# One decode step of attention and MLP: TensorE in a loop of four turns with one V buffer, and announced jumps at two engines' ends

## The chip, the cores and the metric

The kernel runs on one core of a Trainium2 chip. The metric is device microseconds (us) of one execution, median of several. A core has five engines with an instruction stream each: TensorE (PE; its weight loads are listed apart as PEld), VectorE (DVE), ScalarE (ACT), GpSimd (POOL) and SyncE (SP). Transfers between main memory (HBM) and the core's memory (SBUF, 128 partitions) are issued by SyncE or ScalarE and carried out by 16 DMA engines. TensorE writes into eight banks of PSUM. The engines are held together by semaphores alone.

## The reference

One token (Sq = 1) for a batch of 2, model width 448. Layer norm of x; q = xn wq for 16 heads of width 256; attention of two query heads per key/value head (8 of them) over the last 2048 positions of a cache of 8192; output projection wo (4096 to 448). Beside it an MLP on xn (448 to 1792, ReLU, back to 448) whose SiLU gates the attention's output:

```python
s = A(layernorm(x), k_cache, v_cache, wq, wo)     # softmax(q k^T / 16) v, then @ wo
g = silu(relu(layernorm(x) @ w1) @ w2)
return x + s * g
```

All inputs are bf16. K and V windows are 16.8 MB each, wq and wo 3.67 MB each, w1 and w2 1.61 MB each: 44.1 MB to read for little arithmetic.

## The kernel before

**Tiling.** The 16 pairs of batch and key/value head are worked on in four units u of four heads (one batch, half of the heads). A unit's K is one load of 4 MB into `ub[i]`, 128 partitions of 32 KB, a partition holding 64 neighbouring positions of one head; its V likewise. The three buffers `ub[0..2]` take K and V in rotation (`place`, L259).

**A unit's work.** `do_turn` (L268): VectorE transposes K in 32 x 32 blocks, four instructions from `ub` into `kt`. `do_S` (L301): four matmuls put a mask into the bank `sbk`, 32 more add the scores. `do_chain` (L318): VectorE's row maximum, a transpose on TensorE, maximum over groups, broadcast by another matmul, ScalarE's exponential, a transpose on VectorE, 16 small matmuls into `pbk`, and ScalarE's copy to `pt`. `do_sum` (L346): the sums. `do_PV` (L351): 32 matmuls of V by `pt` into `obk`. `do_o` (L361): division by the sum, four matmuls that bring o into columns, a copy into `at_exp`.

**Weights.** wq and w1 have 448 rows. `wq_src` and `w1_src` (L191, L192) cut every row into two halves and lay the 896 halves on all 128 partitions, seven (`SLOTS`) each; `xg`, `par8` and `xr` make the matching arrangement of xn, with zeros where a half doesn't belong. `do_q_mm` (L277) is 28 matmuls into `obk`, `do_q` (L287) brings q for all units into `qz`; `do_H` (L378) is 28 matmuls of w1, `do_F` (L394) 56 of w2 and the gate. wo goes into wq's place (`wqo`) when q is done, in four loads of 20, 8, 2 and 2 rows per partition (`WO_PARTS`), and 128 matmuls into `wbk` consume it in that order at the end.

**Order.** `_Prog` (L23) collects instructions in a list per engine, in the order of the calls in L409 to L483; `run` (L40) writes the lists out straight, with a wait where an instruction needs a later value of a semaphore than its engine has seen. SyncE issues all large loads in one order: wq's first seventh, k0, rest of wq, k1, v0, k2, v1, k3, v2, w1, v3, w2, wo, and then 15 tiny loads `d_probe` (L449), for which it waits at last (L451). A load waits for its buffer: k2 for turn 0, v1 for turn 1, k3 for PV(0), v2 for turn 2, v3 for PV(1). TensorE's order at the units is S(0), S(1), PV(0), S(2), PV(1), PV(2), S(3), H, PV(3), with the chains' small matmuls between; then the two last matmuls of o (L463), F and wo. ScalarE issues the output's transfer and waits for it.

Of the kernel before, what the change touches and what calls it, by code (L numbers as in the profile page):

```python
# [14 lines left out]
class _Op:  # L15
    __slots__ = ("eng", "fn", "deps", "dma", "needed", "value", "sem")

    def __init__(self, eng, fn, deps, dma):
        self.eng, self.fn, self.deps, self.dma = eng, fn, deps, dma
        self.needed, self.value, self.sem = dma, 0, None  # L20


class _Prog:  # L23


    def __init__(self, nc, es):
        self.nc, self.es = nc, es
        self.lists = {PE: [], DVE: [], ACTE: [], SP: [], POOL: []}

    def op(self, eng, fn, deps=()):  # L30
        o = _Op(eng, fn, [d for d in deps if d is not None], False)
        self.lists[eng].append(o)
        return o

    def dma(self, eng, dst, src, deps=()):
        o = _Op(eng, lambda e: e.dma_start(dst, src), [d for d in deps if d is not None], True)  # L36
        self.lists[eng].append(o)
        return o

    def run(self):  # L40
        n = 0
        for ops in self.lists.values():
            for o in ops:
                for d in o.deps:
                    d.needed = True
        for e, ops in self.lists.items():
            sem, count = self.es.enter_context(self.nc.semaphore(f"s_{e}")), 0
            for o in ops:
                if o.dma:
                    n += 1  # L50
                    o.sem, o.value = self.es.enter_context(self.nc.semaphore(f"d_{n}")), 16
                elif o.needed:
                    count += 1
                    o.sem, o.value = sem, count

        def emit(eng, ops):
            seen = {}
            for o in ops:
# [4 lines left out]
                for key, (sem, value) in want.items():  # L63
                    if value > seen.get(key, 0):
                        eng.wait_ge(sem, value)
                        seen[key] = value
                made = o.fn(eng) if o.fn else None
                if o.needed:
                    made.then_inc(o.sem, 16 if o.dma else 1)

        for name, e in (("sync", SP), ("scalar", ACTE), ("gpsimd", POOL), ("vector", DVE), ("tensor", PE)):
            emit(getattr(self.nc, name), self.lists[e])


def bass_recurrent_scan__sliding_block_cached__dense_activation_relu__decode_kernel(
# [22 lines left out]
    NU = 4  # L98
    NT = 64
    UW = NT * DH  # L100
    SLOTS = 7
    HC = HD // 2
    FC = DFF // 2
    WO_PARTS = [20, 8, 2, 2]
    NCOL = D // 4

    es = contextlib.ExitStack()
    with es:
# [5 lines left out]
        def psum(name, shape, dt):  # L114
            return es.enter_context(nc.psum_tensor(name, shape, dt))
# [7 lines left out]
        one_f = named("one_f", [128, 1], F32)  # L123
        par8 = named("par8", [128, 8], F32)
        par2 = named("par2", [128, 2], F32)
        qmask = named("qmask", [128, 4], F32)
        fold = named("fold", [128, 32], BF)
        gsum = named("gsum", [128, 128], F32)
        amask = named("amask", [128, 32], BF)
        x_sb = named("x_sb", [128, D], BF)  # L130
        xg = named("xg", [128, 9 * 128], BF)
# [4 lines left out]
        xr = named("xr", [128, SLOTS * 4], BF)  # L136
        q_n = named("q_n", [128, 512], BF)
        q_t = named("q_t", [128, 512], BF)
        rep4 = named("rep4", [128, 512], BF)
        m8 = named("m8", [1, 8], F32)  # L140
        qz = named("qz", [128, NU * 8 * 32], BF)
        fold8 = named("fold8", [128, 8], F32)
        xr2 = named("xr2", [128, SLOTS * 32], BF)
        h_n = named("h_n", [128, FC // 4], BF)
        h_t = named("h_t", [128, FC // 4], BF)
# [5 lines left out]
        probe = named("probe", [16, 16 * 15], BF)  # L151
        rm = named("rm", [128, 1], F32)
        mrow = named("mrow", [128, 128], F32)
# [5 lines left out]
        pt = [named(f"pt{i}", [128, 512], BF) for i in range(2)]  # L159
# [3 lines left out]
        wqo = named("wqo", [128, 32 * D], BF)  # L163
        assert SLOTS * HC <= 32 * D
        ub = [named(f"ub{i}", [128, UW], BF) for i in range(3)]
        kt = named("kt", [128, UW], BF)
        w1_sb = named("w1_sb", [128, SLOTS * FC], BF)
        w2_sb = named("w2_sb", [128, 14 * D], BF)

        sbk = psum("sbk", [128, 512], F32)  # L170
        pbk = psum("pbk", [128, 512], F32)
        obk = psum("obk", [128, 512], F32)
        fbk = psum("fbk", [128, 512], F32)
        wbk = psum("wbk", [128, 512], F32)
        mbk = psum("mbk", [128, 512], F32)
        hbk = psum("hbk", [128, 512], F32)

        def mbk_ap(lo, n, rows=128):
            return view(mbk, lo, [[1, n]], n=rows)

        def kv_src(u, cache):
            hg, b = divmod(u, 2)
            a = cache[b, 4 * hg:4 * hg + 4, SK - W:SK, :]
            return a.rearrange("h (p t) d -> p h (t d)", t=NT)
# [5 lines left out]

        wq_src = A_wq.rearrange("r (hf c) -> (r hf) c", hf=2).rearrange("(p s) c -> p (s c)", s=SLOTS)  # L191
        w1_src = B_w1.rearrange("r (hf c) -> (r hf) c", hf=2).rearrange("(p s) c -> p (s c)", s=SLOTS)  # L192
        w2_src = B_w2.rearrange("(hf p j) n -> p hf (j n)", hf=2, j=7)
# [5 lines left out]
            base=0, pattern=[[-1, 128]], channel_multiplier=1), [i0])  # L199
        i1 = pr.op(POOL, lambda e: e.memset(ident_f[:, :], 0.0), [p_id])  # L200
# [3 lines left out]
        p_one = pr.op(POOL, lambda e: e.memset(one_f[:, :], 1.0), [p_idf])  # L204
        p_at = pr.op(POOL, lambda e: e.memset(at2[:, :], 0.0))
        p_x2 = pr.op(POOL, lambda e: e.memset(xr2[:, :], 0.0))
# [7 lines left out]
        for e2 in range(2):  # L214
            v_xn = pr.op(DVE, lambda e, e2=e2: e.tensor_scalar(
                out=view(xg, 128 - 127 * e2, [[256, 4], [128, 2], [2, 64]], n=B),
                in0=view(x_sb, 3 * e2, [[1, 4], [0, 2], [SLOTS, 64]], n=B),
                scalar1=st2[0:B, 0:1], scalar2=rstd[0:B, 0:1],
                op0=ALU.subtract, op1=ALU.mult), [v_rs])
        v_par = pr.op(DVE, lambda e: e.tensor_reduce(  # L220
            out=par2[:, :], in_=view(ident, 0, [[1, 2], [2, 64]]), axis=AX.X, op=ALU.add), [p_id])
        v_par8 = pr.op(DVE, lambda e: e.tensor_copy(
            view(par8, 0, [[2, 4], [1, 2]]), view(par2, 0, [[0, 4], [1, 2]])), [v_par])
        v_qm = pr.op(DVE, lambda e: e.tensor_reduce(
            out=qmask[:, :], in_=view(ident, 0, [[32, 4], [1, 32]]), axis=AX.X, op=ALU.add))
# [5 lines left out]
        for i in range(4):  # L231
# [5 lines left out]
        v_gs = pr.op(DVE, lambda e: e.tensor_copy(  # L237
            view(gsum, 0, [[8, 16], [1, 8]]), view(fold8, 0, [[0, 16], [1, 8]])), [v_fold8])
        v_am = pr.op(DVE, lambda e: e.tensor_scalar(
            out=view(amask, 0, [[8, 4], [2, 4], [1, 2]]), in0=view(ident, 0, [[0, 4], [1, 4], [0, 2]]),  # L240
            scalar1=-1.0, scalar2=BIG, op0=ALU.add, op1=ALU.mult), [p_id])

# [4 lines left out]
        for s in range(SLOTS):  # L247
            m_xr = pr.op(PE, mm(mbk_ap(2 * s, 2), xg[0:B, 128 * s + 128:128 * s + 256], ident[0:B, 0:B], s == 0),
# [265 lines left out]
```

## Time and profile before

| what | value |
|---|---|
| median of three runs | 111.34 us (111.2 to 111.41) |
| the profiled execution | 111.39 us, span 109.9 us |
| data read from HBM | 44.11 MB, 401 GB/s over the span |
| mean granted clock of TensorE | 0.761 |
| K transposes on VectorE | 16, 35.6 us, 2279 ns each |
| K loads, V loads | 4 + 4, 4096 KB each |
| matmuls, weight loads | 625 and 625 |

The span runs from the first to the last instruction. A row of a group names line, engine, operation, output from input, count, busy us and mean ns of one, then the idle time before it and what ended it. Nearly all matmuls have L244, the helper's line, so they are told apart by their tiles: `sbk` scores, `obk` PV (and q), `pbk` probabilities, `hbk` and `fbk` MLP, `wbk` output projection, `mbk` small ones. In the slices every digit is the busy share of a fortieth of the span in tenths. The chain that ended last is followed backwards and is no sum of all work.

### The profile page before, as it was taken

To read this page: it belongs to the slowest core of one execution; us is meant where nothing else is said; L and a number is where in the kernel's file an instruction comes from. 1 tells how busy PE (TensorE), PEld (TensorE's weight loads), DVE (VectorE), ACT (ScalarE), POOL (GpSimd) and SP (SyncE) were. 2 spreads that over 40 slices of the span, in tenths; PEclk is the share of its full clock that TensorE was granted. 3 is DMA by queue.
4 is the path that set the end of the run, shared out by engine and by line. 5 is a ranking of instruction groups with operands and counts; after the bars stand their busy time and mean duration, and the time that the engine had idled before them with its cause. 6 is when DMAs were issued, how large, how long until landed. Compare 5 with 4: busy or idle time off the path is not lost.

```text
span 109.9 us, 1444 instructions
## 1 busy us (share of the span) xinstructions
PE 41.1 (37%) x625; PEld 19.2 (17%) x625; DVE 58.0 (53%) x85; ACT 11.0 (10%) x21; POOL 2.5 (2%) x12
## 2 busy tenths in 40 slices
PE   0120000275921302982310059620049913575281
PEld 0000000012211101321210024210013512213270
DVE  1870089937068697016389941348995245123401
ACT  2900000014011200000310000040000022000000
POOL 6200000000000000000000000000000000000000
PEclk9999999999995555599855556995555996569555
DMA  3989999998999899989999998999899988999930
GB/s 59 514 382 465 441 429 429 441 465 382 417 513 405 382 447 489 394 382 465 468 394 405 477 453 382 423 477 429 359 423 482 465 376 373 432 428 416 400 116 7
DMA packets 2706, 44.21 MB, mean 402 GB/s; under 512 B 522, under 2 KB 780, under 8 KB 1292
## 3 DMA queue, kind: packets, MB, share of 16 engines
q1 hardware_dynamic: 2672, 44.11, 94.4%
q8 instruction: 5, 0.08, 0.3%
q10 hardware_dynamic: 28, 0.01, 0.0%
q14 instruction: 1, 0.01, 0.0%
HBM read 44.11 MB, written 0.00 MB: 401 GB/s over the span
## 4 chain that ended last, share of the span: by engine, by line
DMA 49%; PE 22%; DVE 20%; issue 3%; SPq 2%; ACT 1%
DMA wqo<-in_A_wo_dram 31%; DMA wqo<-in_A_wq_dram 18%; DVE kt L273 14%; PE sbk L244 11%; PE obk L244 6%; PE mbk L244 2%; SPq L36 2%; PE wbk L244 1%; DVE ptd L334 1%; DVE rm L319 1%; PE pbk L244 1%; ACT e_sb L329 1%; PE mbk L321 1%; DVE o_sb L363 1%; ACT q_n L288 1%
## 5 line engine op out<-in xcount | busy, mean ns | idle before, releaser
L273 DVE STREAM_TRANSPOSE kt<-ub 128x2048 f32<-128x2048 f32 x16 | 35.6, 2279 | 6.4 <-DMA ub<-in_A_k_cache_dram 6.4
L244 PE MATMUL obk<-ub,pt 128*16 128x512 bf16 x128 | 11.0, 503 | 8.2 <-DMA ub<-in_A_v_cache_dram 8.2
L244 PE MATMUL sbk<-kt,qz 128*32 128x512 bf16 x128 | 12.6, 556 | 0.0
L244 PE MATMUL obk<-wqo,xr 128*4 128x512 bf16 x28 | 3.3, 619 | 15.4 <-DMA wqo<-in_A_wq_dram 13.4
L244 PE MATMUL sbk<-ident,amask 128*32 128x512 bf16 x16 | 2.4, 585 | 16.5 <-DVE kt L273 15.9
L363 DVE TENSOR_SCALAR o_sb<-obk,rs 128x512 bf16<-128x512 f32 x4 | 3.0, 742 | 10.3 <-PE obk L244 10.3
L329 ACT ACTIVATE e_sb<-sbk,bias 128x512 bf16<-128x512 f32 x4 | 2.7, 687 | 53.5 <-DVE bias L328 53.5
L319 DVE TENSOR_REDUCE rm<-sbk 128x1 f32<-128x512 f32 x4 | 2.8, 689 | 9.8 <-PE sbk L244 9.8
L244 PEld LDWEIGHTS obk<-ub,pt 128*16 128x16 bf16 x128 | 3.7, 108 | 14.0 <-DMA ub<-in_A_v_cache_dram 8.4
L244 PEld LDWEIGHTS sbk<-kt,qz 128*32 128x32 bf16 x128 | 4.6, 131 | 6.8 <-issue 6.1
L244 PE MATMUL pbk<-ptd,ident 128*32 128x128 bf16 x64 | 2.0, 264 | 8.5 <-DVE ptd L334 8.5
L244 PE MATMUL wbk<-wqo,at 128*17 128x112 bf16 x128 | 3.4, 296 | 3.0 <-DMA wqo<-in_A_wo_dram 3.0
L334 DVE STREAM_TRANSPOSE ptd<-e_sb 128x512 bf16<-128x512 bf16 x4 | 2.8, 702 | 2.5 <-ACT e_sb L329 2.5
L244 PEld LDWEIGHTS obk<-wqo,xr 128*4 128x4 bf16 x28 | 0.8, 108 | 17.2 <-DMA wqo<-in_A_wq_dram 13.9
L244 PEld LDWEIGHTS sbk<-ident,amask 128*32 128x32 bf16 x16 | 0.5, 113 | 17.1 <-DVE kt L273 16.4
L244 PEld LDWEIGHTS wbk<-wqo,at 128*17 128x17 bf16 x128 | 2.8, 131 | 3.5 <-DVE g_sb L406 2.8
L343 ACT ACTIVATE pt<-pbk 128x512 bf16<-128x512 f32 x4 | 2.4, 598 | 6.7 <-PE pbk L244 6.7
L349 DVE RECIPROCAL rs<-mbk 128x1 f32<-128x1 f32 x4 | 0.7, 169 | 4.1 <-PE mbk L244 4.1
L477 DVE TENSOR_TENSOR tmp<-wbk,g_sb 128x112 f32<-128x112 f32 x1 | 0.3, 274 | 4.7 <-PE wbk L244 4.7
L244 PEld LDWEIGHTS pbk<-ptd,ident 128*32 128x32 bf16 x64 | 1.2, 112 | 8.8 <-DVE ptd L334 8.8
L288 ACT ACTIVATE q_n<-obk 128x512 bf16<-128x512 f32 x1 | 0.6, 597 | 18.8 <-PE obk L244 18.8
L244 PE MATMUL mbk<-one_f,mrow 1*128 1x1 f32 x8 | 1.5, 256 | 2.5 <-DVE mrow L325 2.5
(66 smaller groups left out, 35.9 us busy)
## 6 DMA issues: line engine op xcount, KB each, us to landing
ub<-in_A_k_cache_dram SPq DMA_DIRECT2D x4, 4096.0 KB, 25.4
ub<-in_A_v_cache_dram SPq DMA_DIRECT2D x4, 4096.0 KB, 21.4
w_sb<-in_B_w_dram SPq DMA_DIRECT2D x2, 1568.0 KB, 23.8
wqo<-in_A_wq_dram SPq DMA_DIRECT2D x1, 3072.0 KB, 19.5
wqo<-in_A_wo_dram SPq DMA_DIRECT2D x1, 2240.0 KB, 32.6
wqo<-in_A_wo_dram SPq DMA_DIRECT2D x1, 896.0 KB, 34.5
wqo<-in_A_wq_dram SPq DMA_DIRECT2D x1, 512.0 KB, 3.7
wqo<-in_A_wo_dram SPq DMA_DIRECT2D x2, 224.0 KB, 34.5
```

The lines of the kernel that those rows point to most:

```text
L36: o = _Op(eng, lambda e: e.dma_start(dst, src), [d for d in deps if d is not None], True)
L244: return lambda e: e.matmul(out_ap, lhsT=lhsT, rhs=rhs, start=start, stop=stop, skip_group_check=True, **kw)
L273: st["turn", u, g] = pr.op(DVE, lambda e, lo=lo, hi=hi: e.transpose(k32[:, lo:hi], s32[:, lo:hi]), [dma_of[f"k{u}"], st.get(("S", u - 1))])
L288: a = pr.op(ACTE, lambda e: e.activation(q_n[:, :], obk[:, :], ACT.Copy, scale=SCALE), [st["q_mm"], st["obz"]])
L319: v = pr.op(DVE, lambda e: e.tensor_reduce(out=rm[:, :], in_=sbk[:, :], axis=AX.X, op=ALU.max), [st["S", u]])
L321: m = pr.op(PE, lambda e: e.matmul(mbk_ap(0, 128, 1), lhsT=rm[:, :], rhs=ident_f[:, :], start=True, stop=True, is_transpose=True), [v, p_i ...
L329: a = st["exp", u] = pr.op(ACTE, lambda e: e.activation(e_sb[:, :], sbk[:, :], ACT.Exp, bias=bias[:, 0:1], accum_out=ssum[:, 0:1]), [v, st ...
L334: t = st["ptd", u] = pr.op(DVE, lambda e: e.transpose(ptd[:, :], e_sb[:, :]), [a, st.get(("sp", u - 1))])
L343: st["pt", u] = pr.op(ACTE, lambda e: e.activation(pt[u % 2][:, :], pbk[:, :], ACT.Copy), [o, st.get(("PV", u - 2))])
L349: st["rs", u] = st["mbk"] = pr.op(DVE, lambda e: e.reciprocal(rs[:, u:u + 1], mbk_ap(130, 1)), [st["gs", u]])
L363: st["osb", u] = pr.op(DVE, lambda e: e.tensor_scalar(out=o_sb[:, :], in0=obk[:, :], scalar1=rs[:, u:u + 1], scalar2=None, op0=ALU.mult), ...
L477: v_t = pr.op(DVE, lambda e: e.tensor_tensor(out=tmp[:, :], in0=wbk[:, 0:NCOL], in1=g_sb[:, :], op=ALU.mult), [m_o, st["g"]])
```

## The change

**TensorE.** `_Prog` now takes TensorE's work of a unit as a *turn* of three parts: S, the matmuls of the *previous* unit's o, the chain with the sum; then a part that only the last turn has (H); then PV. `run` emits the instructions of the first turn once, in a loop over four turns, and H inside an `If` in the loop. Since no instruction in the loop can wait for a different value in each turn, the loop's waits are *credits*: a semaphore that another engine or a load raises and that TensorE waits for and lowers again (`kt`, `osb`, `rm`, `mrow`, `ptd`, `va`, `pt`, `vb`). VectorE's first credit for `osb` is given by clearing `o_sb`, GpSimd gives two units' worth of `vb`. The mask is one matmul of 128 columns instead of four of 32. `qz`, `pt` are single buffers now, `qz` is made anew in each turn (`do_qz`).

**Buffers and loads.** K alternates between `ub[0]` and `ub[1]`, V is always in `ub[2]`. A K load waits for S of two units ago, a V load for PV of the unit before; V of units 2 and 3 is loaded in halves, each of which waits for the matching half of PV. w1 goes into wq's place behind wo's first part, so wo's last three loads wait for H also. The probe loads are gone.

**Weights.** wq and w1 lie on 112 partitions, four whole rows each (`NS = 4`): 32 matmuls for q, in two banks, and 16 for H. wq's first load is a quarter, w2 has 14 neighbouring rows per partition.

**Ends.** VectorE's stream and TensorE's each end in a jump to an empty block at the program's end; a branch hint for it stands at the start of VectorE's stream and, on TensorE, behind the loop.

```diff
+        mark = nc.vector.mark_branch_hint_location()
+        for name, e in (("sync", SP), ("scalar", ACTE), ("gpsimd", POOL), ("vector", DVE)):
+            emit(getattr(nc, name), self.lists[e], {})
+        nc.vector.br("dve_end").branch_hint(mark)
+        seen = {}
+        emit(nc.tensor, self.lists[PE], seen)
+        with nc.tensor.Fori(0, len(self.turns)) as i:
+            a, _, b = self.turns[0]
+            assert not any(o.deps for o in a + b)
+            emit(nc.tensor, a, {})
+            with nc.tensor.If(i == len(self.turns) - 1):
+                emit(nc.tensor, self.turns[-1][1], {})
+            emit(nc.tensor, b, {})
+        mark = nc.tensor.mark_branch_hint_location()
+        emit(nc.tensor, self.tail, seen)
+        nc.tensor.br("pe_end").branch_hint(mark)
+        nc.switch_bb("dve_end", parent=None)
+        nc.switch_bb("pe_end", parent=None)
...
+                for name, amount in o.takes:
+                    eng.wait_ge(self.credit[name], amount)
+                    eng.sem_inc(self.credit[name], -amount)
...
-        wq_src = A_wq.rearrange("r (hf c) -> (r hf) c", hf=2).rearrange("(p s) c -> p (s c)", s=SLOTS)
-        w1_src = B_w1.rearrange("r (hf c) -> (r hf) c", hf=2).rearrange("(p s) c -> p (s c)", s=SLOTS)
-        w2_src = B_w2.rearrange("(hf p j) n -> p hf (j n)", hf=2, j=7)
+        wq_src = A_wq.rearrange("(p s) c -> p (s c)", s=NS)
+        w1_src = B_w1.rearrange("(p s) c -> p (s c)", s=NS)
+        w2_src = B_w2.rearrange("(p j) n -> p (j n)", j=NF)
...
-        place = {"k0": 0, "k1": 1, "v0": 2, "k2": 0, "v1": 1, "k3": 2, "v2": 0, "v3": 1}
...
+        def load_k(u):
+            k_in[u] = pr.dma(SP, ub[u % 2][:, :], kv_src(u, A_k_cache), [st.get(("S", u - 2))])
+
+        def load_v(u):
+            free = st.get(("PV", u - 1, 0)), st.get(("PV", u - 1, 1))
+            if u < 2:
+                pr.dma(SP, ub[2][:, :], kv_src(u, A_v_cache), free, gives=("va", 16))
+            else:
+                for half, name in enumerate(("va", "vb")):
+                    lo = half * UW // 2
+                    pr.dma(SP, ub[2][:, lo:lo + UW // 2], kv_src(u, A_v_cache, half * NT // 2, (half + 1) * NT // 2),
+                           [free[half]], gives=(name, 16))
...
+        def do_qz(u, gives=False):
+            hg, b = divmod(u, 2)
+            for par in range(2):
+                pr.op(DVE, lambda e, par=par: e.tensor_tensor(
+                    out=view(qz, 32 * par, [[64, 4], [8, 4], [1, 8]]),
+                    in0=view(fbk, 8 * (16 * hg + 2 * b + par), [[32, 4], [0, 4], [1, 8]]),
+                    in1=view(qmask, 0, [[0, 4], [1, 4], [0, 8]]), op=ALU.mult),
+                    [st["q"], st.get(("S", u - 1)), v_qm], gives=("kt", 1) if gives and par else None)
+
+        def pe_S(u):
+            pr.op(PE, mm(sbk[:, :], amask[:, :], view(ident, 0, [[0, 128], [1, 4]]), True), takes=[("kt", 1)])
+            for wp in range(8):
+                for g in range(4):
+                    st["S", u] = pr.op(PE, mm(
+                        sbk[32 * g:32 * g + 32, :], view(qz, 32 * wp, [[1, 32]]),
+                        view(kt, g * UW // 4 + 64 * (wp // 2) + wp % 2, [[256, 16], [2, 32]]), False, wp == 7,
+                        tile_position=(0, 32 * g)))
+
+        def pe_oT(u):
+            takes = [("osb", 1)]
+            for dblk in range(2):
+                for ts in range(2):
+                    lo = 256 * ts + 128 * dblk
+                    st["oT", u] = pr.op(PE, mm(cols(tbk, 8 * dblk, 8), o_sb[:, lo:lo + 128],
+                                               fold[:, 8 * ts:8 * ts + 8], dblk == 0 and ts == 0, ts == 1), takes=takes)
+                    takes = []
+
+        def pe_chain(u):
+            st["rmT", u] = pr.op(PE, lambda e: e.matmul(cols(mbk, 0, 128, 1), lhsT=rm[:, :], rhs=ident_f[:, :],
+                                                        start=True, stop=True, is_transpose=True), takes=[("rm", 1)])
+            st["mT", u] = pr.op(PE, lambda e: e.matmul(cols(mbk, 128, 1), lhsT=mrow[0:1, :], rhs=ident_f[0:1, 0:1],
+                                                       start=True, stop=True, is_transpose=True),
+                                takes=[("mrow", 1)])
+            takes = [("ptd", 1)]
+            for g in range(4):
+                for Q in range(4):
+                    st["sp", u] = pr.op(PE, mm(pbk[32 * Q:32 * Q + 32, 128 * g:128 * g + 128],
+                                               ident[:, 32 * g:32 * g + 32], view(ptd, 8 * Q, [[32, 16], [1, 8]]),
+                                               g == 0, True, tile_position=(0, 32 * Q)), takes=takes)
+                    takes = []
+            st["gs", u] = pr.op(PE, mm(cols(mbk, 130, 1), gsum[:, :], ssum[:, 0:1], True, True))
+
+        def pe_PV(u):
+            takes = [("va", 16), ("pt", 1)]
+            for k in range(NT // 2):
+                g = k % 4
+                if k == NT // 4:
+                    takes = [("vb", 16)]
+                o = pr.op(PE, mm(obk[32 * g:32 * g + 16, :], view(pt, 16 * k, [[1, 16]]),
+                                 ub[2][:, 512 * k:512 * k + 512], k < 4, k >= 28, tile_position=(0, 32 * g)),
+                          takes=takes)
+                takes = []
+                st["PV", u, k // (NT // 4)] = o
+
+        def pe_H():
+            deps = [d_w1]
+            for s in range(NS):
                 for i in range(4):
+                    lo = W1_AT + s * DFF + i * HCOL
+                    st["H"] = pr.op(PE, mm(hbk[32 * i:32 * i + 17, 0:HCOL], xr[0:XP, 32 * s:32 * s + 17],
+                                           wqo[0:XP, lo:lo + HCOL], s == 0, s == NS - 1,
+                                           tile_position=(0, 32 * i)), deps)
                     deps = []
+
+        def dve_chain(u, between=None):
+            pr.op(DVE, lambda e: e.tensor_reduce(out=rm[:, :], in_=sbk[:, :], axis=AX.X, op=ALU.max),
+                  [st["S", u]], gives=("rm", 1))
+            if u:
+                dve_at(u - 1)
             v = pr.op(DVE, lambda e: e.tensor_reduce(
+                out=m8[:, :], in_=view(mbk, 0, [[1, 8], [8, 16]], n=1), axis=AX.X, op=ALU.max, negate=True),
+                [st["rmT", u]])
+            pr.op(DVE, lambda e: e.tensor_copy(
+                view(mrow, 0, [[8, 16], [1, 8]], n=1), view(m8, 0, [[0, 16], [1, 8]], n=1)), [v], gives=("mrow", 1))
+            v = pr.op(DVE, lambda e: e.tensor_copy(bias[:, :], cols(mbk, 128, 1)), [st["mT", u]])
+            a = pr.op(ACTE, lambda e: e.activation(
+                e_sb[:, :], sbk[:, :], ACT.Exp, bias=bias[:, 0:1], accum_out=ssum[:, 0:1]), [v, st.get(("gs", u - 1))])
             if between:
                 between()
+            pr.op(DVE, lambda e: e.transpose(ptd[:, :], e_sb[:, :]), [a, st.get(("sp", u - 1))], gives=("ptd", 1))
+            pr.op(ACTE, lambda e: e.activation(pt[:, :], pbk[:, :], ACT.Copy), [st["sp", u]], gives=("pt", 1))
+            st["rs", u] = pr.op(DVE, lambda e: e.reciprocal(rs[:, u:u + 1], cols(mbk, 130, 1)), [st["gs", u]])
+
+        def dve_osb(u):
+            pr.op(DVE, lambda e: e.tensor_scalar(
+                out=o_sb[:, :], in0=obk[:, :], scalar1=rs[:, u:u + 1], scalar2=None, op0=ALU.mult),
+                [st["PV", u, 1], st["rs", u]], gives=("osb", 1))
+
+        def dve_at(u):
+            hg, b = divmod(u, 2)
+            st["at", u] = pr.op(DVE, lambda e: e.tensor_tensor(
+                out=view(at_exp, 128 * b + 64 * hg, [[8, 8], [4, 2], [1, 4]]),
+                in0=view(tbk, 0, [[1, 8], [8, 2], [0, 4]]),
+                in1=view(qmask, 0, [[0, 8], [0, 2], [1, 4]]), op=ALU.mult), [st["oT", u], v_qm])
+
...
+        for u in range(NU):
+            pr.turn()
+            pr.within(0)
+            pe_S(u)
+            pe_oT(u - 1)
+            pe_chain(u)
+            pr.within(1)
+            if u == NU - 1:
+                pe_H()
+            pr.within(2)
+            pe_PV(u)
+            if u == 0:
+                do_qz(0, True)
+                load_k(2)
+                load_v(1)
+                dve_chain(0, lambda: do_turn(1, 0, 1))
+                do_qz(1)
+                do_turn(1, 1, 4, True)
+            else:
+                if u > 1:
+                    do_qz(u)
+                    do_turn(u, gives=True)
+                dve_osb(u - 1)
+                dve_chain(u)
+                if u == 1:
+                    load_k(3)
+                    load_v(2)
+                    d_w1 = pr.dma(SP, wqo[0:XP, W1_AT:W1_AT + NS * DFF], w1_src, [st["q_mm"]])
+                if u == 2:
+                    load_v(3)
+        pr.after()
+        d_w2 = pr.dma(SP, w2_sb[:, :], w2_src)
+        d_wo, j0 = [], 0
+        for n in WO_PARTS:
+            d_wo.append((j0, pr.dma(SP, wqo[:, j0 * D:(j0 + n) * D], wo_src[:, j0 * D:(j0 + n) * D],
+                                    [st["q_mm"], st["H"] if j0 else None])))
+            j0 += n
...
-        d_probe = [pr.dma(SP, probe[0:k, 16 * (k - 1):16 * k], A_x[0, 0, 0:16 * k].rearrange("(k c) -> k c", c=16))
-                   for k in range(1, 16)]
-        pr.op(SP, None, d_probe)
```

## The prediction

> **What bounds the kernel now.** I read the page's head, slices and DMA queues first, then the chain that ended last, then SyncE's waits, then busy time by stretch of the end.
>
> ```profile
> PE 41.1 (37%) x625; PEld 19.2 (17%) x625; DVE 58.0 (53%) x85; ACT 11.0 (10%) x21; POOL 2.5 (2%) x12
> ...
> DMA  3989999998999899989999998999899988999930
> ...
> DMA packets 2706, 44.21 MB, mean 402 GB/s; under 512 B 522, under 2 KB 780, under 8 KB 1292
> ...
> q1 hardware_dynamic: 2672, 44.11, 94.4%
> q8 instruction: 5, 0.08, 0.3%
> ...
> DMA 49%; PE 22%; DVE 20%; issue 3%; SPq 2%; ACT 1%
> ```
>
> No engine is above 53%, while the DMA row is 8 or 9 tenths from the second slice to the 38th and SyncE's queue alone fills 94.4% of the 16 engines. So the transfers set the time. The chain's 20% on VectorE and 22% on TensorE lie beside a full DMA row and are not a price list. Of the instruction row I note five packets of 0.08 MB: divided by TensorE's 1250 matmuls and weight loads that is 64 bytes each, so I read it as TensorE's code coming in during the run, on the same 16 engines as the data.
>
> ```profile
> SPq L36 <- DVE kt L273: 53.8, 3, 19.8
> SPq L36 <- PE obk L244: 5.2, 1, 5.2
> ...
> 22.99 0.54 SPq L36 DMA_DIRECT2D ub<-in_A_k_cache_dram  x1
> 43.38 0.53 SPq L36 DMA_DIRECT2D ub<-in_A_v_cache_dram  x1
> 49.15 0.54 SPq L36 DMA_DIRECT2D ub<-in_A_k_cache_dram  x1
> 64.36 0.54 SPq L36 DMA_DIRECT2D ub<-in_A_v_cache_dram  x1
> ```
>
> SyncE waits long for free buffers, but the DMA row shows no hole behind these waits: two 4 MB loads (about 9.7 us each) are always ahead. The stretches, in us, end with granted clock, DMA share, GB/s:
>
> ```profile
> 1.86:14.07 12.21, 0.94 (x11) 0.38 (x11) 4.88 (x19) 3.39 (x6) 1.50 (x4) 1.00 1.01 419
> 14.07:21.41 7.34, 0.00 (x1) 0.01 (x2) 7.34 (x4) 0.00 (x0) 0.00 (x0) 1.00 1.03 443
> ...
> 104.50:105.00 0.50, 0.50 (x32) 0.50 (x27) 0.00 (x0) 0.00 (x0) 0.00 (x0) 0.50 0.79 262
> 105.00:105.50 0.50, 0.50 (x36) 0.50 (x28) 0.00 (x0) 0.00 (x0) 0.00 (x0) 0.50 0.40 110
> 105.50:106.00 0.50, 0.39 (x19) 0.14 (x8) 0.00 (x0) 0.00 (x0) 0.00 (x0) 0.50 0.32 105
> 106.00:106.50 0.50, 0.29 (x16) 0.29 (x20) 0.00 (x0) 0.00 (x0) 0.00 (x0) 0.50 0.23 80
> 106.50:107.00 0.50, 0.50 (x32) 0.50 (x27) 0.00 (x0) 0.00 (x0) 0.00 (x0) 0.50 0.06 8
> 107.00:107.50 0.50, 0.50 (x24) 0.20 (x12) 0.00 (x0) 0.00 (x0) 0.00 (x0) 0.50 0.14 33
> ```
>
> The end is the second thing to see. The engines do not finish together: full until 104.5, then a ragged tail to about 107.1. The tail holds 0.5 x (0.79 + 0.40 + 0.32 + 0.23 + 0.06 + 0.14) = 0.97 us of all sixteen, so an even finish would come at about 105.5. Some few engines are about 1.6 us late, and the last matmuls wait for them (48 of them start at 106.21, released by wo):
>
> ```profile
> 106.21 1.35 PE L244 MATMUL wbk<-wqo,at 128*17 128x112 bf16 x48 [0.32 <-DMA wqo<-in_A_wo_dram]
> ```
>
> **The change part by part.** The sum is made against the profiled execution: 111.39 us, that is 109.9 of span and 1.49 around it; it lies 0.05 above the median of 111.34.
>
> *One V buffer, K loads that wait for S, V2 and V3 in halves.* No bytes are added; the question is whether the DMA row gets holes. At 430 GB/s (mean of 419 and 443) a 4.19 MB load takes 9.75 us: after wq at 21.4, k1 lands near 31.2, v0 40.9, k2 50.7, v1 60.4, k3 70.2, v2 at 81.07 (its row, an engine late), w1 (1.6 MB, 3.7) near 84.8, v3 at 94.57 (its row). New issue times: k2 waits for S(0) instead of turn 0, so near 30.7 instead of 22.99; v0 keeps the queue until 40.9. v1 now waits for PV(0): v0 by 42, plus 3.59 for 32 matmuls at the slow clock, 45.6; k2 keeps the queue until 50.7. Queued behind v1 is k3 (S(1) ends near 47 to 50, needed by 60.4). v2's halves wait for halves of PV(1): 63.3 and 65.1, queue full until 70.2. v3's: the first at 78 to 79 (v2's first half and pt(2)), the second at 81.07 + 1.8 = 82.9; w1 covers the first until 84.8 and v3's first half the second until 89.7. Behind it stand w2 and wo; wo's last three parts also wait for H (near 93), with w2 and 20 rows of wo queued until 103.8. The smallest margin is 5 us. Cost taken: 0; without that cover, each us of lateness costs a us.
>
> *The loop on TensorE.* Turn 3 is the only one whose lateness reaches the end, since V's landings set PV(0) to PV(2) anew. S(3) starts after PV(2) at 82.9, takes 4.0 cold, the chain from row max to the sum 4.7 (86.91 to 91.66 before), H about 1, so pt is ready at about 93, before v3's second half. PV(3) has only its second half left after 94.57, so it ends at 96.4 against 98.2 now. Then o, its transposes and at2: before, at2 was done at 100.7; now about 98.4 (1.8 from PV, 0.6 for one copy in place of two). TensorE then waits for wo until 103.84. Jumps, register instructions and eight semaphore decrements per turn are in no row; bounds: 0, and the longest issue gap of a row, 2.1 us a jump. Turn 3 has room for some 4 to 5. Taken: 0. VectorE's qz moves ahead of each K transpose (two of 0.28 us), q becomes twice as wide (about +0.3 us once), one mask matmul replaces four; all of it beside full transfers. [...]
>
> *wq and w1 on 112 rows instead of 128.* The same bytes, 3.67 and 1.61 MB, in rows of 32 and 14 KB per partition. The trace has no transfer of 112 rows. If the sixteen engines get 7 rows each, the cost is 0. If the fullest get 8, as with 128 rows, they need 8/7 of the time: 8.5 us of wq (3.67 MB at 430) and 3.75 of w1 give 12.3/7 = 1.75 us. Less than nothing is excluded, since no byte goes away and the share was already 1.0. I take 1.2, nearer the upper end: the tail rows show that what one engine has too much is not taken over by others (0.40 busy at 105 while the rest is done), so unevenness is paid in the end. [...]
>
> *Code fetches.* By the diff TensorE's code becomes some 80 instructions before the loop, 230 in it and 380 after, about 700 for the 1250 and some waits of now; in proportion to the five packets two or three remain. Fewer fetches do not help in proportion: if a fetch puts one engine behind, and nothing later lets it catch up (the DMA row has no hole), a single early one leaves that engine late to the end. Bounds: 0 (as many late engines, if the loop fetches again in each turn), and -1.55 (107.1 to 105.5, no late engine at all). Since I expect at least one fetch, I stay near 0 and take -0.25. [...]
>
> *Small parts.* The probe loads go: 15 loads of 120 packets behind all of wo, on a queue that waits for nothing after; 0, covered by the output transfer, which ends the span. V's halves add packets, w2 in one piece saves some: ±0.1. The first wq piece grows from 0.52 to 0.92 MB, so k0 is 0.9 us later; turn 0 then ends at 23.9, before q's matmuls do (24.16): 0. The end jumps lie beside the output's landing.
>
> Sum: 111.39 + 1.2 - 0.25 = 112.34, less 0.05 to the median: 112.3.
>
> **Rivals.** (1) *Even rows.* 112 divides by 16; then 0 instead of 1.2: 111.1, its own range 110.9 to 111.4. For it: the arithmetic; against: no row. (2) *No engine late, even rows* — the other side: no code fetch meets the data, the ragged tail closes, 111.34 - 1.55 = 109.8. It decides as soon as the fullest engine's surplus from 112 rows is under 1.35 us; for it speaks that 1.55 us of the tail are engines, not bytes; against, that one fetch suffices to keep most of it. (3) *Uneven rows, no engine late*: 111.34 + 1.2 - 1.55 = 111.0. (4) *The loop or the V buffer becomes the bound*: jumps of more than 5 us in turn 3, or V loads issued late by more than the 5 us of margin, or 112-row transfers at a far lower rate; from 113.3 up. Against: the margins above. (5) *The changes do nothing*: as 1, without the quarter.
>
> **How the numbers follow.** Chances: forecast 0.42 (111.7 to 113.0), even rows 0.22, no engine late 0.14, both effects 0.10, loop or loads 0.12. The measurement tells 0.2%, 0.22 us. Faster: 0.14 + 0.10 + half of rival 1 = 0.35; same 0.10; slower 0.42 + 0.12, some 0.55. The range goes from 109.7 (rival 2) to 113.3 and leaves out most of rival 4. The likeliest case's own range is 111.7 to 113.0.
>
> **What would show it.** The instruction row falls from 5 packets to 1 or 2 (if it rises, the loop fetches anew). The tail from 104 on: long and shallow if rows are uneven, steep if no engine is late. wq landed at 21.4 now: 22.4 or later means uneven rows. The DMA row must stay at 8 or 9; a hole after 40 or 60 refutes the margins. TensorE should still wait for wo before its last 128 matmuls. The prediction is wrong if 112-row loads land as early as now, or if the tail closes.

## The result and the profile after

The changed kernel takes 120.0 us (median of six runs, 119.32 to 122.7), the kernel before beside it 111.45 us (111.2 to 112.77). The ratio is 1.0735, interval 1.0672 to 1.0798: slower by some 8 us. The ratio compares the means of the runs and leaves out the one of 122.7 us, which fell into a slower state that some runs of other kernels here show too (114.51 us of the kernel before). 112.3 was forecast with a range up to 113.3, so the sign held and the size did not. The profiled execution is 119.32 us with a span of 117.9, against 111.39 and 109.9.

The page of the changed kernel, in the lines that answer to those shown of before, and below the DMA row the bytes moved in each slice (a slice is 2.95 us):

```profile
PE 45.3 (38%) x602; PEld 19.1 (16%) x602; DVE 58.2 (49%) x82; ACT 10.6 (9%) x20; POOL 2.3 (2%) x12
...
DMA  3989899989899998989999899999999999999920
GB/s 90 400 368 523 356 275 267 350 253 489 367 489 400 434 456 373 489 378 478 411 434 456 378 478 389 412 428 439 336 311 293 384 428 424 425 445 412 389 73 6
DMA packets 2575, 44.16 MB, mean 375 GB/s; under 512 B 314, under 2 KB 572, under 8 KB 700
...
q1 hardware_dynamic: 2544, 44.11, 94.2%
q8 instruction: 3, 0.05, 0.2%
...
DMA 13%; PE 4%; DVE 0%; issue 0%
```

The engines are as little loaded as before, and the DMA row is still full without a hole. Yet the row below it sinks twice: to 250 to 350 GB/s in the sixth to ninth slice, where wq's rest is loaded, and to 290 to 340 in slices 29 to 31, where w1 is. The same 44.11 MB go through at 375 instead of 402 GB/s. Here a full busy share says that the engines hold packets, not that the packets move at full rate.

The same by stretches, ends in us, with granted clock, DMA share and GB/s at the end of the line: k0, wq's rest, k1, then a stretch with w1 and one with v3's halves.

```profile
5.50:15.40 9.90, 1.03 (x8) 0.15 (x8) 0.82 (x5) 0.00 (x0) 0.00 (x0) 1.00 1.01 411
15.40:26.70 11.30, 0.00 (x0) 0.00 (x0) 8.89 (x4) 0.00 (x0) 0.00 (x0) 1.00 0.96 275
26.70:36.00 9.30, 6.98 (x61) 2.20 (x61) 1.89 (x4) 1.88 (x2) 0.00 (x0) 1.00 0.99 426
83.30:92.20 8.90, 5.08 (x49) 1.51 (x49) 4.36 (x3) 0.00 (x0) 0.00 (x0) 0.54 1.01 307
92.20:101.00 8.80, 5.28 (x60) 2.25 (x56) 3.97 (x9) 1.38 (x3) 0.00 (x0) 0.65 0.99 421
```

wq's rest (3072 KB then, 2688 KB now) took 7.34 us at 443 GB/s before; now 11.3 us at 275. A 128-partition load just before it runs at 411, one just behind at 426. The share is 0.96 to 1.01 throughout. The stretch of w1 in the kernel before:

```profile
78.60:84.30 5.70, 3.23 (x32) 1.15 (x36) 5.23 (x3) 0.00 (x0) 0.00 (x0) 0.50 1.09 466
```

The trace's record of packets says the same from the inside. A packet here is one row on one of the 16 engines; the last columns are the landing on the last engine, in us from the span's start:

```
               wq's rest: packets          w1: packets                 wq lands  wo lands
before         24576 B  912 ns             12544 B  472 ns               21.36    107.15
after          24576 B 1463 (1073-1653)    14336 B  774 (571-1192)       26.68    115.14
```

The wq packets carry the same bytes as before and take 1.6 times as long; a w1 packet takes 774, where 14336/12544 x 472 = 539 ns is an estimate from its size and the packets before. wq lands 5.3 us later, k1 5.0 (36.09 against 31.07), and this stays through k2, v1 and k3 (76.11 against 71.45, 4.66). By w2 the difference is 8.1 (106.45 against 98.34), by wo 8.0, and that is the growth of the span, 117.9 less 109.9.

The end of the kernel, in stretches of 1 us:

```profile
111.00:112.00 1.00, 0.04 (x4) 0.08 (x8) 0.00 (x0) 0.00 (x0) 0.00 (x0) 0.50 0.96 364
112.00:113.00 1.00, 1.00 (x48) 1.00 (x52) 0.00 (x0) 0.00 (x0) 0.00 (x0) 0.50 0.39 142
113.00:114.00 1.00, 1.00 (x44) 0.75 (x33) 0.00 (x0) 0.00 (x0) 0.00 (x0) 0.50 0.13 43
114.00:115.00 1.00, 0.91 (x41) 0.87 (x40) 0.00 (x0) 0.00 (x0) 0.00 (x0) 0.50 0.04 16
```

```profile
99.13 14.92 DMA wqo<-in_A_wo_dram
114.05 0.04 issue
114.09 1.45 PE wbk L279 x41
```

The ragged tail is still there, and longer: the share falls to 0.39 at 112, and the last 41 matmuls start at 114.09, when the last engine has landed its part of wo's second load (114.05). Of wo's last load, the middle engine is done at 112.9 and the last one at 115.14, 2.2 us apart.

TensorE's own order cost nothing. Its matmuls at the borders of turns 0 to 1 and 2 to 3 and at the end:

```profile
46.10 3.59 PE L279 MATMUL obk<-ub,pt 128*16 128x512 bf16 x32 [3.26 <-PEq L97]
50.18 0.50 PE L279 MATMUL sbk<-ident,amask 128*128 128x512 bf16 x1 [0.49 <-PEq L97]
...
87.12 1.89 PE L279 MATMUL obk<-ub,pt 128*16 128x512 bf16 x16 [3.95 <-PEq L97]
88.94 0.61 PE L279 MATMUL sbk<-ident,amask 128*128 128x512 bf16 x1
...
111.95 3.55 PE L279 MATMUL wbk<-wqo,at 128*17 128x112 bf16 x128 [3.97 <-DMA wqo<-in_A_wo_dram]
```

A jump back costs at most 0.49 us (`PEq L97` is TensorE's wait for a credit), once nothing at all, and TensorE then stands idle for 3.97 us before wo. SyncE's waits for buffers are long, 5 for PV (`obk`), 2 put down to o's matmuls (`tbk`), 1 for H (`hbk`). The two are the K loads, which by the code wait for S, just ahead of o's matmuls:

```profile
SPq L42 <- PE obk L279: 46.3, 5, 15.5
SPq L42 <- PE tbk L279: 35.5, 2, 33.0
SPq L42 <- PE hbk L279: 8.4, 1, 8.4
```

but all of them end ahead of the queue's emptying: the wait for H, the last, ends at 99.1, while w2 ahead of it lands at 106.45.

### The profile page after: what moved, and what is told of

Read it like the earlier page. It is cut to its first block, busy times and chain, and to the rows that moved or that the text cites. A ratio compares the mean times of both kernels' runs of the same rounds, so it can differ in the third digit from the quotient of the medians.

```text
span 117.9 us, 1423 instructions
## 1 busy us (share of the span) xinstructions
PE 45.3 (38%) x602; PEld 19.1 (16%) x602; DVE 58.2 (49%) x82; ACT 10.6 (9%) x20; POOL 2.3 (2%) x12
## 3 DMA queue, kind: packets, MB, share of 16 engines
q1 hardware_dynamic: 2544, 44.11, 94.2%
HBM read 44.11 MB, written 0.00 MB: 374 GB/s over the span
## 5 line engine op out<-in xcount | busy, mean ns | idle before, releaser
L279 PE MATMUL obk<-ub,pt 128*16 128x512 bf16 x128 | 14.8, 627 | 22.5 <-PEq L97 22.5
L279 PE MATMUL obk<-wqo,xr 112*17 112x512 bf16 x16 | 2.5, 614 | 21.0 <-DMA wqo<-in_A_wq_dram 21.0
L279 PE MATMUL sbk<-kt,qz 128*32 128x512 bf16 x128 | 10.5, 482 | 0.0
L279 PEld LDWEIGHTS sbk<-kt,qz 128*32 128x32 bf16 x128 | 3.7, 112 | 6.1 <-issue 4.8
L279 PE MATMUL hbk<-wqo,xr 112*17 112x512 bf16 (+1 forms) x32 | 4.3, 601 | 0.0
L279 PEld LDWEIGHTS obk<-wqo,xr 112*17 112x17 bf16 x16 | 0.5, 116 | 22.5 <-DMA wqo<-in_A_wq_dram 21.9
L330 DVE TENSOR_SCALAR q_n<-hbk 128x512 bf16<-128x512 f32 x1 | 0.7, 692 | 4.4 <-PE hbk L279 4.4
L279 PE MATMUL sbk<-ident,amask 128*128 128x512 bf16 x4 | 2.3, 574 | 1.2 <-PEq L97 1.2
```

The source lines that it names most:

```text
L279: return lambda e: e.matmul(out_ap, lhsT=lhsT, rhs=rhs, start=start, stop=stop, skip_group_check=True, **kw)
L330: v = pr.op(DVE, lambda e: e.tensor_scalar(out=view(q_n, 256, [[512, 2], [1, 256]]), in0=view(hbk, 0, [[256, 2], [1, 256]]), scalar1=SCALE ...
```

## The experiments

The theory after the result: loads into 112 partitions run at a lower rate, and this alone makes the 8 us. The rivals: the V buffer and the credits delay loads; the loop or the jumps bring code fetches at a bad moment; or the engines are unevenly loaded, and it is this that costs.

**loop128: everything but the 112 rows.** wq, w1 and w2 lie on 128 partitions as before (w1 in a buffer of its own); loop, credits, one V buffer and both jumps stay.

```diff
-        wq_src = A_wq.rearrange("(p s) c -> p (s c)", s=NS)
-        w1_src = B_w1.rearrange("(p s) c -> p (s c)", s=NS)
-        w2_src = B_w2.rearrange("(p j) n -> p (j n)", j=NF)
+        wq_src = A_wq.rearrange("r (hf c) -> (r hf) c", hf=2).rearrange("(p s) c -> p (s c)", s=SLOTS)
+        w1_src = B_w1.rearrange("r (hf c) -> (r hf) c", hf=2).rearrange("(p s) c -> p (s c)", s=SLOTS)
+        w2_src = B_w2.rearrange("(hf p j) n -> p hf (j n)", hf=2, j=7)
...
-                    d_w1 = pr.dma(SP, wqo[0:XP, W1_AT:W1_AT + NS * DFF], w1_src, [st["q_mm"]])
+                    d_w1 = pr.dma(SP, w1_sb[:, :], w1_src)
```

> The changed kernel with wq, w1 and w2 laid out as in the kernel before (wq and w1 on 128 partitions, w1 in a buffer of its own, 28 matmuls for q and for H); loop, credits, one V buffer, halves, K loads that wait for S, jumps and hints stay. Theory R (the loss is the 112-row loads alone: wq's rest landed at 26.68 instead of 21.36, w1 cost some 2 us more): 111.2, between 110.6 and 111.8, and wq lands near 21.4. Rival L (the loop, the V buffer or the new waits cost part of the 8.5 us): 113 to 118, with wq at 21.4 and the lateness appearing behind a turn.

Measured: 111.61 us (111.35 to 112.02), before 111.5; ratio 1.0016, interval 0.999 to 1.0043. The whole 8 us are gone. The edit also takes back what goes with the 112 rows: q's matmuls in two banks, wq's larger first piece, w2's order of rows, and the wait of wo's last loads for H. That none of these costs is read from the traces of the changed kernel, where the time is lost in the packets of the two loads, and the wait for H ends at 99.1, before w2 ahead of wo's last loads has landed. From its page, and the stretches of wq's rest and of w1:

```profile
DMA  3989999999999999989999999999999999999930
...
q8 instruction: 2, 0.03, 0.1%
```

```profile
13.10:21.00 7.90, 0.00 (x0) 0.00 (x0) 6.60 (x3) 0.00 (x0) 0.00 (x0) 1.00 1.07 460
78.70:84.40 5.70, 3.18 (x25) 0.83 (x29) 3.93 (x3) 0.00 (x0) 0.00 (x0) 0.50 1.01 428
```

460 and 428 GB/s where the changed kernel has 275 and 307. Loop, credits, single V buffer, halves, jumps and the missing probes are worth nothing together within that interval, neither loss nor gain: the last part of wo lands at 107.15 us, to a hundredth where it landed before.

**straight and nohints: the changed kernel without loop and jumps, and without the jumps alone.** Both keep the 112 rows.

```diff
-        with nc.tensor.Fori(0, len(self.turns)) as i:
-            a, _, b = self.turns[0]
...
+        for a, h, b in self.turns:
+            emit(nc.tensor, a, seen)
+            emit(nc.tensor, h, seen)
+            emit(nc.tensor, b, seen)
         emit(nc.tensor, self.tail, seen)
-        nc.tensor.br("pe_end").branch_hint(mark)
```

The diff is straight's; nohints takes out only the two marks, the two `br` with their hints and the two empty blocks.

> The changed kernel with TensorE's four turns written out one after the other instead of a loop, and without the jumps and hints at the ends; 112-row loads, credits and buffers stay. Theory R: within 0.7 of the changed kernel's 120.0, the instruction row back at 4 to 6 packets instead of 3. Rival L: 113 to 117, if the loop's jumps are what costs.

> The changed kernel without the two end jumps and their hints; the loop stays. Theory R: 119.7 to 120.7; if the hints save a code fetch, one packet more in the instruction row (4, or an 8 KB one for VectorE near 55) and, if it meets an engine that is on time, the last loads up to 0.7 later. A rival in which the hints themselves cost: 119.5 or less.

Measured: straight 121.26 us (120.73 to 121.94), ratio 1.0872, interval 1.0792 to 1.0952; nohints 121.11 us (120.37 to 122.18), ratio 1.0897, interval 1.0817 to 1.0976. Both lie above what was expected, 119.3 to 120.7. Of TensorE's code, straight has five packets of 16 KB, nohints two (the instruction rows of their pages, in this order):

```profile
q8 instruction: 5, 0.08, 0.3%
```

```profile
q8 instruction: 2, 0.03, 0.1%
```

So five packets or two make the same time, and the loop is not the cause. That both lie 1.1 to 1.3 us above the changed kernel shows in one place: w1's packets take 979 and 969 ns in the middle instead of 774, and the stretch from 83.30 to 92.20 moves 244 and 256 GB/s instead of 307. wq's stretch is the same in all three (275, 275 and 278 from 15.40 to 26.70). What makes w1's packets differ between programs that issue the same load was not settled; more on it at w1112.

**straight128 and loop128nohints: the same two undone with 128 rows.** loop128 with the edits of straight and of nohints.

Straight128:

```diff
-        with nc.tensor.Fori(0, len(self.turns)) as i:
...
+        for a, h, b in self.turns:
```

loop128nohints:

```diff
-        nc.vector.br("dve_end").branch_hint(mark)
...
-        nc.tensor.br("pe_end").branch_hint(mark)
```

> All of the change but the 112-row layout, the loop and the end jumps: weights on 128 partitions, TensorE's turns written out, one V buffer, credits, halves. Theory R: 111.3 to 112.0, wq landing at 21.4, 5 or 6 code packets and several late engines as in the kernel before; straight (121.26) minus this is then the price of 112 rows with this code, 9.3 to 10. Rival B (the one V buffer and the new waits cost, and the loop gave it back): 112.3 to 113.5.

> As loop128 (111.61) without the end jumps and hints. With 112 rows, dropping them cost 1.1 us (121.11 against 120.0), and VectorE's 8 KB code packet came back at 63.4. If a late engine costs by itself: 111.6 to 111.9, since one engine is 1.3 us late already and the 8 KB packet makes a second one only 0.7 late. If the hints save something else: 112.5.

Measured: straight128 111.6 us (111.41 to 112.1), ratio 0.9984, interval 0.9949 to 1.0019; loop128nohints 111.71 us (111.15 to 113.33), ratio 0.9977, interval 0.9937 to 1.0017. The six kernels side by side, medians in us:

```
              loop and jumps    loop alone    written out
112 rows          120.0           121.11        121.26
128 rows          111.61          111.71        111.6
```

The price of the 112 rows is 8.4, 9.4 and 9.7 us. The medians come from several series, in which the kernel before lies between 111.45 and 111.82; by the ratios to it the three prices are 8.0, 10.3 and 9.9. Loop and jumps together are worth nothing with 128 rows and some 1 to 2 us with 112, where the intervals of the changed kernel and of straight just overlap.

**wq112 and w1112: one of the two loads on 112 rows, the other on 128.** Both are loop128 with one load changed, and the matmuls that use it. wq112:

```diff
+        wq_src = A_wq.rearrange("(p s) c -> p (s c)", s=NS)
...
+        d_wq.append(pr.dma(SP, wqo[0:XP, HD:NS * HD], wq_src[:, HD:NS * HD]))
```

w1112, with w2's rows in the order that the changed kernel has:

```diff
+        w1_src = B_w1.rearrange("(p s) c -> p (s c)", s=NS)
...
+                    d_w1 = pr.dma(SP, w1_sb[0:XP, :], w1_src)
```

> Loop, jumps and V buffer of the changed kernel, w1 on 128 rows as in loop128, only wq on 112 rows. Theory (each load on 112 rows pays for itself): wq lands about 5 us later than in loop128, at 26.5 instead of 21.7, nothing later adds to it: 116.4 us, between 115.9 and 117.0. Rival (the two loads make each other worse, because one leaves engines uneven for the other): wq alone costs as much less as w1 alone does, both sums together clearly under the 8.4 us of the changed kernel against loop128, 115.5 or less here. If 112 rows of wq cost what the rows of widths say (217 against 364 GB/s, with their latency in them), 3.67 MB cost up to 6.8 us: 118.4.

> The other half: wq on 128 rows as in loop128, only w1 on 112 rows (with w2 in the changed kernel's order of rows, 128 partitions as before). Theory: w1's packets take about 770 ns as in the changed kernel, w1 costs 2 to 3 us and nothing else does: 113.6 to 114.6 us, so that wq112 and this one together give the 8.4 us. Rival (uneven engines are what makes w1 slow): with engines as even as in loop128 the w1 packets take about 600 ns, 112.3 to 113.0 us. If the order of w2's rows mattered, the w2 load would land later by more than w1 does.

Measured: wq112 116.48 us (115.88 to 116.71), ratio 1.0451, interval 1.0401 to 1.05; w1112 115.8 us (115.49 to 116.19), ratio 1.0367, interval 1.0313 to 1.0421. The stretches of wq's rest and of w1 in wq112, then in w1112:

```profile
15.30:25.40 10.10, 0.00 (x0) 0.00 (x0) 8.89 (x4) 0.00 (x0) 0.00 (x0) 1.00 1.02 290
83.20:88.80 5.60, 3.02 (x25) 0.84 (x29) 3.95 (x3) 0.00 (x0) 0.00 (x0) 0.50 1.01 427
```

```profile
13.10:21.00 7.90, 0.00 (x0) 0.00 (x0) 6.09 (x3) 0.00 (x0) 0.00 (x0) 1.00 1.07 460
78.70:89.00 10.30, 5.48 (x57) 1.66 (x53) 5.21 (x4) 0.00 (x0) 0.00 (x0) 0.57 1.04 255
```

Each load is slow by itself and leaves the other alone. Against loop128's 111.61, wq costs 4.9 us, as the theory had it, and w1 4.2, more than its 2 to 3. Their sum is 9.1, against 8.4 for both together; the intervals are about 0.55 us wide to either side, so this is additive within what can be told.

The rival that uneven engines alone make w1 slow expected about 600 ns a packet; they take 924. This was no clean test, for the engines were not quite as even as in loop128: of the sixteen landings of k3, two come over 1 us behind the first in w1112 (70.76 and 71.67 against 69.44), one in loop128 (71.29). Straight128 decides it: there four come so late, and w1's packets on 128 rows take 473 ns; and in widths, below, 112 rows are slow with no load ahead of them. Late engines may still make a load on 112 rows slower than it is by itself. The four traces that have one fall in that order: one such landing of k3 in the changed kernel (774 ns), two in w1112 and nohints (924 and 969), three in straight (979). No run changes this alone, so it stays a guess. w1 also slows what travels beside it: of the 16 KB packets of V's halves one in ten takes 981 ns or more in w1112, 619 in loop128 (the middle is 611 to 613 in both).

**widths: the load by itself.** Nothing but seven loads from the K cache, one after the other has landed, each with rows of 24 KB per partition; attention, MLP and output projection are left out and zeros are written. `full` has 128 partitions, `most` 112 from partition 0, `upper` 112 from partition 16, `pitch` 112 with rows 32 KB apart in HBM (as in the change), `threeq` 96, `half` 64; `sevens` are seven loads of 16 partitions that are queued together. Each was run once, in one execution.

```diff
+        load("full", 0, 0, 128)
+        load("most", 1, 0, 112)
+        load("upper", 2, 16, 112)
+        load("pitch", 3, 0, 112, 64)
+        load("threeq", 4, 0, 96)
+        load("half", 5, 0, 64)
+        load("sevens", 6, 0, 112, T, 16)
```

> Loads alone, each waiting for the one before, no computing (the output is zeros): rows of 24 KB from the K cache onto 128 partitions (full), 112 from partition 0 (most), 112 from partition 16 (upper), 112 with the rows 32 KB apart in memory (pitch), 96 (threeq), 64 (half), and 112 as seven loads of 16 (sevens). Theory R1 (the number of destination partitions decides): full 3.1 MB at 410 to 440 GB/s, about 7.3 us plus some 2 of latency; most, upper and pitch alike, 2.75 MB in 9 to 11 us instead of 6.4, packets longer than full's 912 ns though they have the same size; half at about half the rate (1.6 MB in 7 us). [...] Rival R2 (the rows' distance in memory decides): most as fast per byte as full, pitch alone slow. Rival R3 (the mixture with other loads decides): all but half at full rate.

The transfers of widths, KB and us from issue to landing, and the stretches of `full`, `most` and `half`, which end with granted clock, DMA share and GB/s:

```profile
full<-in_A_k_cache_dram SPq DMA_DIRECT2D x1, 3072.0 KB, 9.8
most<-in_A_k_cache_dram SPq DMA_DIRECT2D x1, 2688.0 KB, 13.6
upper<-in_A_k_cache_dram SPq DMA_DIRECT2D x1, 2688.0 KB, 13.9
pitch<-in_A_k_cache_dram SPq DMA_DIRECT2D x1, 2688.0 KB, 12.3
...
threeq<-in_A_k_cache_dram SPq DMA_DIRECT2D x1, 2304.0 KB, 12.9
half<-in_A_k_cache_dram SPq DMA_DIRECT2D x1, 1536.0 KB, 10.6
```

```profile
4.20:12.70 8.50, 0.00 (x0) 1.00 0.93 364
14.10:26.20 12.10, 0.00 (x0) 1.00 0.87 217
...
54.00:65.60 11.60, 0.00 (x0) 1.00 0.88 193
67.00:76.20 9.20, 0.00 (x0) 1.00 0.79 171
```

112 partitions take 3.8 us longer than 128, with an eighth fewer bytes. It is not the pitch of the rows in HBM (12.3, even a little less), not which 112 (13.6 and 13.9), and needs no neighbour in the queue. The middle packet of 24 KB, from the trace:

```
128 rows  912 ns    112 rows 1601 (upper 1625, pitch 1473)    96 rows 1844
64 rows  1928 ns    16 rows  3424 (the first of the seven loads 2318)
```

From the first packet's start to the last one's end, `most`, `upper` and `pitch` need 11.0 to 12.3 us, more than the 9 to 11 expected; so the number of partitions decides, as R1 had it, at a higher price. The engines share the load evenly: the sixteen land their parts of `most` between 25.32 and 26.66, less than one packet apart, and its 112 packets took 177.2 us together, 11.1 for each engine out of 11.8. What grew is the time of a packet.

Against the 912 ns with 128 rows the same 24 KB take 1.8 times as long with 112 rows, 2.0 with 96 and 2.1 with 64; of the loads of 16 rows the six that were queued behind another take 3.75 times, the first 2.5. Which engine takes which of the 112 rows, and why the packets take longer, was not shown.

**early: a jump announced early to bring code in.** loop128, with TensorE's last 80 matmuls in a block of their own, reached by a jump that is announced at TensorE's start; meant to take the last code packet away from the wo loads.

```diff
+        early = nc.tensor.mark_branch_hint_location()
...
+        emit(nc.tensor, self.tail[:110], seen)
+        nc.tensor.br("pe_rest").branch_hint(early)
+        nc.switch_bb("pe_rest")
-        emit(nc.tensor, self.tail, seen)
+        emit(nc.tensor, self.tail[110:], seen)
```

> loop128 with one more jump on TensorE, into the block of the last 80 of wo's matmuls, announced at the very start of its stream. If an announced target is fetched when it is announced, the code packet of 40.1 us moves to the first two us, v0 to w2 land without a late engine (v0 at 41.1 instead of 42.3), one packet near 102 stays; last wo load at about 106.9 to 107.2 and the time 111.2 to 111.6. If the announcement does not bring the block: as loop128, 111.6.

Measured: 112.44 us (112.25 to 114.06), ratio 1.0073, interval 1.0034 to 1.0111: slower, by about 0.8 us, where both cases expected 111.6 or less. The chain at its end:

```profile
106.16 1.35 PE wbk L292 x42
107.51 0.88 issue
108.39 0.36 PE wbk L292 x5
```

With everything landed, TensorE stops for 0.88 us before its last five matmuls, which it does not in loop128. The packets in the trace: one of 16 KB at 40.21 as in loop128, the other at 105.99 (loop128: 102.41). The announcement did not move the early packet, it moved the late one to where TensorE waits. That the 0.88 us are that wait is likely but was not shown: the packet itself ends at 107.0.

No kernel tried is faster than the one before beyond its interval.

## Why the prediction was right or wrong

**The bound: right.** Transfers set the time before and after; the latest engine's part of wo's second load releases the last matmuls in both (landed at 106.16, matmuls from 106.21; now 114.05 and 114.09).

**One V buffer, K loads that wait for S: 0, right.** loop128 carries all of it at a ratio of 1.0016. The margin that the prediction found smallest, 5 us, holds: v1 is issued at 49.73, and k2 ahead of it lands on the first engine at 54.82; the DMA row has no hole.

**The loop: 0, right.** 0.49 us at the one border where it can be seen, 3.97 us idle before wo. The announced bound of 2.1 us a jump was far too wide.

**wq and w1 on 112 rows: this step failed.** The prediction took 1.2 between bounds of 0 and 1.75 and measured is 8.4 (against loop128): 4.9 for wq and 4.2 for w1 alone. Without saying so, the step assumed that a packet of a given size takes a given time, 24 KB in 912 ns, so that the only question was whether an engine gets seven rows or eight. So 8/7 became the upper bound. What was shown instead: the engines share the rows evenly (the landings of `most`, 25.32 to 26.66), which by the step would cost 0, and with 112 rows the packets themselves take 1.6 times as long (wq's 1463 ns against 912). Why they do stays open. "The trace has no transfer of 112 rows" was true, and the bounds should have been as wide as that ignorance.

**"Less than nothing is excluded, since no byte goes away and the share was already 1.0": right as a sign, but from a wrong reading.** The share stayed at 1.0 while the rate fell from 443 to 275 GB/s. The share was read as a rate.

**Code fetches, -0.25: not there.** The packets fell from five to three, with 128 rows to two, and the last engine was no earlier for it: loop128's wo lands at 107.15 as before. The reason given for staying near 0, that one packet is enough, holds: in loop128 a packet of 1060 ns at 40.14 is followed by one engine that ends v0 at 42.3, where the others end it at 40.3 to 41.1, and up to wo's first load one landing of each load stays about 1 us behind the other fifteen. The gain that was bounded at -1.55 supposes no packet at all in the full stretch, and no kernel here had that.

**The small parts: 0, within the measurement.** They are all in loop128 but for wq's larger first piece, q's width and w2 in one piece, which no run tries without 112 rows. One size was off: k0 lands 2.2 us later (16.23 against 14.05), not 0.9; wq's first piece ahead of it, a load on 112 rows too, lands at 6.13 against 4.40.

**The rivals.** Even rows, no engine late, both effects and "nothing" all took a seventh of the two loads' time, 1.75 us, as the most that 112 rows can cost, and fell with the step. The fourth rival held the case in a clause, "112-row transfers at a far lower rate; from 113.3 up", with a chance of 0.12 shared with two others, and without a price. It had its own sign, wq's landing, but the sign was set for the other question: 22.4 or later would mean uneven rows, and 26.68 came.

**The signs.** The instruction row: 3, where 1 or 2 were named. The tail: long and shallow, as named for uneven rows. No hole: right. TensorE waits for wo: right. The two signs named for being wrong, an early landing and a closed tail, both looked for a smaller cost; neither looked for a larger one.

## What to carry to other kernels

When the DMA row is full, ask for the rate in each stretch and the time of one packet, not for the share: a layout that keeps all bytes and all engines busy cost 38% of the rate in its stretch here (275 against 443 GB/s). In a kernel bound by loads, keep weights on 128 partitions even at the price of split rows and zero-padded vectors; 112 cost 4.9 us on a 3.67 MB load and 4.2 on one of 1.61 MB, and everything that the simpler layout saved on the engines lay beside the transfers. And where the trace has no row for a kind of transfer, the upper bound is the worst row that could be like it, not the arithmetic of even shares.

## What the runs showed of the hardware that was not expected

- A load of 24 KB a partition into 112 partitions takes longer than one into 128 that carries more: 13.6 us against 9.8 from issue to landing. 96 partitions take 12.9 us for 2304 KB, 64 take 10.6 for 1536 KB.
- The busy share of the DMA engines is 0.96 while they move 275 GB/s, and 1.03 where the kernel before moves 443.
- The same w1 load on 112 rows costs between 774 and 979 ns a packet in programs that differ only in loop, jumps, wq's layout or w1's buffer (774, 924, 969, 979). What sets it is open.
- The announced jumps at the ends went with the loss of a packet of 8 KB of code that stands at 53.38 in the kernel before, at 63.41 in nohints and 58.09 in loop128nohints, and neither in the changed kernel nor in loop128. Which of the two jumps does it was not separated. With 128 rows it bought nothing (111.61 us with the jumps, 111.71 without).
- A loop on TensorE, by the prediction's estimate some 230 instructions, run four times, showed no new code packet between its first turn and the end: 46.19 and then 113.01 in the changed kernel.
